# Attention into an MLP on one core: a third buffer for the exps, q and k of the first batch ahead of its values, and the first beacon keys on GpSimd's DMA queue

## The chip, the cores and the metric

The kernel runs on one core of one Trainium2 chip. The metric is the device time of one execution in microseconds (us), as the median of several runs; lower is better. All times inside an execution are counted from the start of the profiled span.

## The reference

Eight batches of causal attention with 16 extra keys ("beacons") ahead of the sequence feed a two-layer MLP. The 4608 rows of the MLP are the 8 x 576 tokens; a row is the 8 heads x 64 values of one token.

```python
B, H, S, Nb, D = (8, 8, 576, 16, 64)
k_all = np.concatenate([beacon_k, k], axis=2)
v_all = np.concatenate([beacon_v, v], axis=2)
scores = scale * np.matmul(q, k_all.transpose(0, 1, 3, 2))
scores = np.where(causal, -1000000000.0, scores)   # the beacons are always visible
a = softmax(scores)
x = np.matmul(a, v_all).transpose(0, 2, 1, 3).reshape(B * S, H * D)
h = x @ w_in                                        # 512 -> 2048
out = (h * sigmoid(1.702 * h)) @ w_out              # 2048 -> 512
```

Inputs and output are float32; the kernel works in float16 with float32 sums.

## The kernel before, in words

**Steps.** A step i is one batch and one pair of heads: 8 x 4 = 32 steps, step i belonging to batch i // 4. For a step, TensorE computes transposed scores (`qk_chunk`, L331) in four chunks of 512, 480, 464 and 208 columns for each of the two heads, into a ring of two PSUM tiles `s`. ScalarE takes the exp of each chunk (`exp_chunk`, L344) into the step's tile `E`, of which there are two. VectorE or GpSimd sets the blocks on the diagonal to zero (`mask_chunk`, L360 or L367). TensorE multiplies by the values (`av_both`, L430, for steps 0 to 3; `av_half`, L401, after that). The values stand beside a column block of ones, so the same matmuls give the softmax sums. VectorE turns these sums round, inverts them, turns them back and multiplies (`z_turn`, `z_recip`, `z_back`, `norm`), which gives `xT`, the transposed input of the MLP.

**MLP.** It runs in nine groups of 512 tokens. `mlp1` (L516) is 64 matmuls into 16 PSUM tiles, each followed by a gelu on ScalarE (L528); `mlp2` (L538) is four blocks of 16 matmuls, whose results are copied out (`mlp2_out`, L549 on ScalarE, L551 on VectorE) and stored. All matmul outputs other than scores share a ring of four PSUM tiles `u`. For every group but the last ones the order on TensorE is written out by `chain` (L939): the 64 matmuls of `mlp1` of the group, then the next attention steps with one block of `mlp2` in each. The first group comes after step 4; its first block of `mlp2` comes in step 7, between the score chunks 1 and 2.

**Loads.** Loads that change the type go through GpSimd's DMA queue, called the software queue here: q and k of the first two batches (`load_qk6`, L146), the values (`load_v`, L218 and L221), `w_in` in four pieces (`load_w1`, L228), q and k of later batches (`load_qk`, L115), `w_out` in four pieces (`load_w2`, L235). The program gives that queue eight semaphores in turn, so a load waits on GpSimd until the eighth load before it has landed. In the first batch q and k of heads 0 and 1 come without a cast on the queues of SyncE and ScalarE (`load_f32`, L155) and are cast in SBUF (`cast_f32`, L165); so do the beacon keys of the first two batches (`load_bk6`, `cast_bk6`, L173 and L179). The beacon keys of the other batches are eight small transfers on SyncE (`load_bk`, L128) and one cast (`cast_bk`, L136). q and k of batches 0 and 1 are transposed on TensorE (`tr_pe`, L190) and copied out (`tr_pe_out`, L198). For later batches VectorE transposes 32 x 32 squares (L253), VectorE or GpSimd put them in order (`tr_order`, L262), and SyncE writes them to DRAM and reads them back in place (L272, L279).

**Planner.** Apart from `chain`, `issue` (L964) decides the order and the engine. It goes through all `Work` items with assumed durations, takes the one that can start first (ties by the due time `key`), and picks the engine that would end first, plus a `BIAS`. What an item `needs` becomes a semaphore wait through the data; what stands in `after` only orders the planner's choice, and puts no wait into the program between two engines.

Of the kernel before, what the change touches and what calls it, by code (L numbers as in the profile page):

```python
# [16 lines left out]
def kernel(  # L17
# [46 lines left out]
    tp = ctx.enter_context(tc.tile_pool(name="tp", bufs=2))  # L64
    ep = ctx.enter_context(tc.tile_pool(name="ep", bufs=2))
    op_ = ctx.enter_context(tc.tile_pool(name="op", bufs=3))
# [15 lines left out]
    def make_keep():  # L82

        nc.gpsimd.affine_select(
            out=keep,
            in_=keep,
            compare_op=ALU.is_ge,
            fill=0.0,
            base=0,
            pattern=[[1, P + Nb]],  # L90
            channel_multiplier=-1,
        )

    w1t = cst.tile([P, NKP, DFF], F16, tag="w1", name="w1")
# [55 lines left out]

    def load_f32(w, eng):

        s = op_.tile([P, 2, S], F32, tag="O", name="O")
        stg[w] = s
        dict(SP=nc.sync, ACT=nc.scalar)[eng].dma_start(  # L155
            out=s.rearrange("p x s -> p (x s)")[0:TP, 0 : 2 * TR * D].rearrange(
                "p (h c) -> p h c", h=2
            ),
            in_=(q, k)[w][0, 0:2].rearrange("h (p t) d -> p h (t d)", t=TR),
        )  # L160

    def cast_f32(w, eng):
        if 0 not in nat6:
            nat6[0] = gp.tile([TP, 2, H, TR * D], F16, tag="g", name="g")
        copy[eng](  # L165
            out=nat6[0][:, w, 0:2, :].rearrange("p h c -> p (h c)"),
            in_=stg[w].rearrange("p x s -> p (x s)")[0:TP, 0 : 2 * TR * D],
        )

    def load_bk6(b):  # L170
        s = sp.tile([P, DMODEL], F32, tag="osb", name="osb")
        stg["b", b] = s
        nc.sync.dma_start(  # L173
            out=s[0:Nb, :].rearrange("n (h d) -> n h d", d=D),
            in_=beacon_k[b].rearrange("h n d -> n h d"),
        )
# [143 lines left out]
    scs = {}  # L320

    def qk_chunk(i, ci):
        b, p = divmod(i, NPAIR)
        qT, kT = qTs[b % 2], kTs[b % 2]
        sc = pss.tile([P, 2, 512], F32, tag="s", name="s")
        scs[(i, ci)] = sc
        o = 0
        for (j, a, e) in CH[ci]:
            for x in range(2):
                r = 64 * x  # L330
                nc.tensor.matmul(  # L331
                    sc[:, x, o : o + e - a],
                    kT[r : r + 64, p, j * P : (j + 1) * P],
                    qT[r : r + 64, p, a:e],
                    start=True,
                    stop=True,
                )
            o += e - a

# [233 lines left out]
    class Buf:  # L573
# [4 lines left out]
    rings = dict(  # L578
        n0=2, n1=2, sq=2, t0=2, t1=2, d0=4, d1=4, qT0=1, qT1=1, kT0=1, kT1=1, vb0=1, vb1=1, s=2, E=2, u=4, O=3,
        zt=2, rt=2, rz=2, xT=RING, g=2, osb=3,  # L580
    )
    SEM, QS = 0.1, 0.1
    SPL, CAP = 2.0, 2.0
    NBOTH = 4
    HWQ = 3

    def use(buf, *ws):
        buf.users += ws
# [4 lines left out]
    placed = {}  # L593
    bkB = None
    pk = {}
    trp = {}
    mkeep = Work("POOL", 0.3, -4.95, make_keep)
    midn = Work("POOL", 0.6, -5.95, lambda: make_identity(nc, ident))

    bk6, stw, cst0 = {}, {}, {}  # L600
    stb = {w: Buf("O") for w in (1, 0, "bk")}
    stw[1] = Work("SP", 0.6, -9, lambda: load_f32(1, "SP"), alloc=stb[1], dma=0.7)
    stw[0] = Work("ACT", 0.6, -9, lambda: load_f32(0, "ACT"), alloc=stb[0], dma=0.7, after=[stw[1]])
    for b in range(NB2):
        ob = Buf("osb")
        x = Work("SP", 0.6, -8 + b, lambda b=b: load_bk6(b), alloc=ob, dma=0.1, after=[stw[1]])
        bk6[b] = Work(
            dict(ACT=0.6, DVE=0.6) if b else dict(ACT=0.6), 0, (-8, 1.5)[b],
            lambda eng, b=b: cast_bk6(b, eng), [x],
        )  # L610
        use(ob, bk6[b])
    g0 = Buf("g")
    for w in (1, 0):
        cst0[w] = Work(
            {("DVE", "ACT")[w]: 0.85}, 0, -8.5 - 0.1 * w, lambda eng, w=w: cast_f32(w, eng),
            [stw[w]],
        )
        use(stb[w], cst0[w])

    def first_loads(b):  # L620
        k0 = 4 * b
        kl = (-6, -4.4)[b]
        gb6 = g0 if b == 0 else Buf("g")
        lds = {(0, 1): cst0[1], (0, 0): cst0[0]} if b == 0 else {}
        got = []
        for (h0, h1) in ((2, 4), (4, H)) if b == 0 else ((0, 4), (4, H)):
            for w in (1, 0):
                x = Work(
                    "POOL", 0.7, kl + 0.1 * h0 + 0.02 * (1 - w) + (h0 == 4),
                    lambda b=b, h0=h0, h1=h1, w=w: load_qk6(b, h0, h1, w),  # L630
                    alloc=None if got else gb6, dma=0.37 * (h1 - h0), after=got[:1],
                )
                got.append(x)
                for p in range(h0 // 2, h1 // 2):
                    lds[(p, w)] = x
        if b == 0:
            for x in cst0.values():
                x.after.append(got[0])
        x = None
# [29 lines left out]
        pk[b] = y  # L669
        if b == 0:  # L670
            bk6[1].after.append(pk[(0, 0, 1)])

    for b in range(B):
# [5 lines left out]
        for g in range(2) if b >= NB2 else ():  # L679
            for w in (1, 0):  # L680
# [17 lines left out]
                for e in range(2):  # L698
                    cp.append(Work(
                        dict(DVE=0.8, POOL=1.3), 0, k0,  # L700
                        lambda eng, b=b, g=g, w=w, e=e: tr_order(b, g, w, e, eng),
                        tr, alloc=tb_ if e == 0 else None, after=cp[:1],
                    ))
                use(sb_, *cp)
                need = []
                if w == 1:
                    if bkB is None:
                        ld4 = [
                            Work(
                                "SP", 1.2, -6 + x, lambda x=x: load_bk(x),  # L710
                                alloc=stb["bk"] if x == 0 else None, dma=0.2,
                            )
                            for x in range(HG)
                        ]
                        for x, y in zip(ld4, ld4[1:]):
                            y.after.append(x)
                        bkB = [Work(dict(ACT=0.85, DVE=0.85, POOL=0.9), 0, 3, cast_bk, ld4)]
                        use(stb["bk"], *bkB)
                    need = [Work(
                        "DVE", 0.25, k0, lambda b=b, g=g: tr_beacon(b, g),  # L720
                        bkB, after=cp[:1],
                    )]
# [12 lines left out]
                placed[(b, g, w)] = pl  # L735
        kv = 4 * b - 1.5 if b >= NB2 else (-5.5, -3)[b]
        for j in range(NJ):
# [26 lines left out]
    avp = {}  # L764
    BIAS = dict(DVE=0.5), dict(ACT=0.7)
    avs = []
    evs = {}
    for i in range(NSTEP):
# [4 lines left out]
        ready = {}  # L773
        for c in range(len(CH)):
            s_ = Buf("s")
            qk_ = Work(
                "PE", CHW[c] / 2400 + 0.05, i + (0, 0.01, 0.4, 0.41)[c],
                lambda i=i, c=c: qk_chunk(i, c),
                [pk[(b, p, 0)], pk[(b, p, 1)], pk[b]] if b < NB2
                else [placed[(b, hf, 0)], placed[(b, hf, 1)]],  # L780
# [6 lines left out]
            ex = Work(  # L787
                "ACT", 0.17 + 2 * CHW[c] / 1200, i + (0, 0.01, 0.4, 0.41)[c],
                lambda i=i, c=c: exp_chunk(i, c), [qk_],
# [6 lines left out]
            nm = sum(1 for (j, a, e) in CH[c] if a == s0s[j])  # L796
            mk = Work(
                dict(DVE=0.46 * nm, POOL=0.41 * nm), 0, i + 0.3,
                lambda eng, i=i, c=c: mask_chunk(i, c, eng), [ex, mkeep],
            )  # L800
            use(Eb, mk)
            for (j, a, e) in CH[c]:
# [5 lines left out]
        if i < NBOTH:  # L808
            for z in (1, 0):
                for half in range(2):  # L810
# [3 lines left out]
                    av = Work(  # L814
                        "PE", sum(hi - lo for (j, lo, hi, col) in mm) / 2400 + 0.15,
                        i + 1.05 + 0.2 * (1 - z) + 0.1 * half,
                        lambda i=i, half=half, z=z: av_both(i, half, z),
                        [r for j in js for r in ready[j]] + vb_, alloc=ub[(half, z)],
                        after=avs[-1:],
# [68 lines left out]

    trp[(0, 1, 1)].after.append(qks[(0, 1)])
    bkB[0].after.append(exps[0][3])  # L890

# [72 lines left out]
    def issue():  # L964
# [7 lines left out]
        while todo:  # L972
            best = None
            for w in todo:
# [18 lines left out]
                for a in w.after:  # L993
                    t = max(t, a.t0)
                eng = min(w.opts, key=lambda e: max(t, free[e]) + w.opts[e] + BIAS[t > 45].get(e, 0))
                t = max(t, free[eng])
# [11 lines left out]
            if eng == "PE":  # L1008
                d += 0.1 * (w.mode != mode)
                mode = w.mode  # L1010
            if w.key >= 1e6 and t < 7:
                d = 0.43
# [65 lines left out]
```

The softmax here doesn't subtract the row's maximum and nothing guards it: scores larger than these inputs give would overflow.

## Time and profile before

| what | value |
|---|---|
| median of 5 runs | 367.94 us (367.52 to 368.38) |
| the profiled execution | 368.5 us |
| its span | 366.8 us |
| TensorE busy | 353.6 us (96%), 2349 matmuls |
| VectorE, ScalarE, GpSimd busy | 249.2 (68%), 228.1 (62%), 152.7 us (42%) |
| software queue (q0) | 18.19 MB |
| queues of SyncE and ScalarE (q1) | 24.55 MB |
| first matmul of the first `mlp1` | at 35.62 us |
| first matmul of the first `mlp2` | at 59.43 us |

The profile has a page with the busy time of each engine (PE is TensorE, PEld its weight loads, DVE VectorE, ACT ScalarE, POOL GpSimd, SP SyncE), the same in 40 slices of the span with the clock that TensorE was granted, the chain of work that ended last, followed back from the end, and the costliest groups of instructions. A line such as `E<-s` reads: the tile E is written from the tile s. Answers of the trace narrow this to a window of time, to an engine or to a tile. A landing is the moment at which all parts of a transfer are done.

### The profile page before, as it was taken

The numbers are of one execution on the slowest core, as the hardware profiler recorded it, in microseconds if no ns is written. First come the engines' busy times: TensorE is split into PE (matmuls) and PEld (weight loads), VectorE is DVE, ScalarE is ACT, GpSimd is POOL, SyncE is SP. The second block draws the span as 40 slices with busy tenths as digits, with TensorE's granted clock in tenths as the row PEclk, the third lists the DMA queues.
The fourth block names the chain that finished last, engine by engine and source line by source line (L and its number), as shares of the span: only waits on it lengthen the run. The fifth ranks groups of instructions, "written<-read, shape, count | busy, mean of one in ns | idle before, by whom it ended". The sixth has DMA issues, their size and how long they took to land.

```text
span 366.8 us, 6133 instructions
## 1 busy us (share of the span) xinstructions
PE 353.6 (96%) x2349; PEld 176.8 (48%) x2349; DVE 249.2 (68%) x421; ACT 228.1 (62%) x335; POOL 152.7 (42%) x264
## 2 busy tenths in 40 slices
PE   7689999999999999999999999999999999999995
PEld 3365444444444444544445864544444454444442
DVE  5547499999999986999599949981995183010021
ACT  4569787648765776677857675677658734616200
POOL 9578567593368244743376236710430010000000
PEclk9969999999999999999999999999999999999999
DMA  9999999994689645894489447921100011000012
GB/s 143 149 206 188 187 236 234 224 110 99 191 231 178 132 126 146 129 168 136 124 113 139 139 141 144 134 87 32 59 30 29 2 57 57 2 29 29 30 57 86
DMA packets 69788, 43.41 MB, mean 118 GB/s; under 512 B 42624, under 2 KB 62080, under 8 KB 69760
## 3 DMA queue, kind: packets, MB, share of 16 engines
q0 software_dynamic: 49152, 18.19, 48.7%
q1 hardware_dynamic: 20400, 24.55, 21.4%
q8 instruction: 18, 0.29, 0.3%
q10 hardware_dynamic: 208, 0.29, 0.3%
q14 instruction: 10, 0.08, 0.1%
HBM read 44.60 MB, written 16.61 MB: 167 GB/s over the span
## 4 chain that ended last, share of the span: by engine, by line
PE 86%; DVE 4%; DMA 3%; ACT 3%; POOL 2%; issue 1%; DVEq 0%; POOLq 0%
PE u L516 34%; PE u L538 34%; PE u L401 9%; PE s L331 7%; DMA g<-in_q_dram 3%; ACT E L344 2%; PE u L430 1%; POOL vb L221 1%; DVE xT L489 1%; PE u L190 1%; DVE rz L480 1%; DVE zt L470 1%; DVE osb L551 1%; DVE O L459 1%; POOL g L146 1%
## 5 line engine op out<-in xcount | busy, mean ns | idle before, releaser
L344 ACT ACTIVATE E<-s 128x1024 f16<-128x1024 f32 (+3 forms) x128 | 103.4, 865 | 48.8 <-PE s L331 46.6
L538 PE MATMUL u<-w,g 128*128 128x512 f16 x576 | 129.2, 379 | 0.6 <-DVE O L459 0.6
L516 PE MATMUL u<-xT,w 128*128 128x512 f16 (+1 forms) x640 | 126.0, 358 | 0.0
L528 ACT ACTIVATE g<-u 128x512 f16<-128x512 f32 x144 | 85.2, 597 | 42.8 <-PE u L516 42.5
L367 POOL TENSOR_SCALAR_AFFINE_SELECT E<-E 128x256 f16<-128x256 f16 (+2 forms) x148 | 63.6, 448 | 84.3 <-ACT E L344 84.1
L516 PEld LDWEIGHTS <-w 128*128 128x128 f16 x640 | 62.1, 98 | 61.3 <-issue 0.9
L538 PEld LDWEIGHTS <-g 128*128 128x128 f16 x576 | 54.5, 98 | 65.4 <-issue 3.6
L551 DVE COPY osb<-u 128x512 f32<-128x512 f32 x30 | 20.5, 683 | 65.3 <-PE u L538 65.0
L459 DVE COPY O<-u 128x240 f32<-128x240 f32 (+1 forms) x84 | 34.8, 439 | 24.5 <-PE u L401 22.1
L262 POOL COPY t<-sq 128x576 f16<-128x576 f16 x21 | 26.7, 1272 | 49.2 <-DVE sq L253 41.5
L401 PE MATMUL u<-E,vb 128*128 128x240 f16 x392 | 46.8, 266 | 0.2
L489 DVE TENSOR_TENSOR xT<-O,rz 64x576 f16<-64x576 f32 x56 | 44.2, 790 | 0.8
L470 DVE STREAM_TRANSPOSE zt<-O 64x576 f32<-64x576 f32 x56 | 43.1, 770 | 1.4
L401 PEld LDWEIGHTS <-vb 128*128 128x128 f16 x392 | 32.2, 98 | 17.3 <-issue 7.6
L331 PE MATMUL s<-qT,kT 64*128 64x80 f16 (+5 forms) x384 | 37.2, 285 | 3.3 <-ACT E L344 2.3
L253 DVE STREAM_TRANSPOSE sq<-n 128x576 f16<-128x576 f16 x48 | 34.9, 747 | 6.7 <-DMA n<-in_k_dram 6.4
L221 POOL DMA_DIRECT2D vb<-in_v_dram x40 | 34.3, 865 | 3.4 <-DMA w<-in_moe_w_in_dram 2.8
L262 DVE COPY t<-sq 128x576 f16<-128x576 f16 x27 | 27.4, 1015 | 0.3
L331 PEld LDWEIGHTS <-kT 64*128 64x128 f16 x384 | 13.3, 94 | 27.6 <-issue 20.0
L480 DVE STREAM_TRANSPOSE rz<-rt 128x576 f32<-128x576 f32 x32 | 24.4, 763 | 0.6
L459 ACT COPY O<-u 128x336 f32<-128x336 f32 (+1 forms) x28 | 10.7, 429 | 2.8 <-PE u L401 2.7
L1043 PE MATMUL u<-wu 128*128 128x512 f16 x29 | 10.4, 461 | 1.3 <-DVE wu L1036 1.3
(44 smaller groups left out, 124.9 us busy)
## 6 DMA issues: line engine op xcount, KB each, us to landing
out_dram<-osb SPq DMA_DIRECT2D x36, 256.0 KB, 2.1
d<-t SPq DMA_DIRECT2D x12, 296.0 KB, 2.8
kT<-d SPq DMA_DIRECT2D x12, 296.0 KB, 3.5
n<-in_k_dram POOLq DMA_DIRECT2D x12, 288.0 KB, 5.2
n<-in_q_dram POOLq DMA_DIRECT2D x12, 288.0 KB, 6.2
d<-t SPq DMA_DIRECT2D x12, 288.0 KB, 2.6
qT<-d SPq DMA_DIRECT2D x12, 288.0 KB, 3.2
vb<-in_v_dram POOLq DMA_DIRECT2D x24, 128.0 KB, 5.7
```

Of the source, the lines that this page charges most:

```text
L221: nc.gpsimd.dma_start(out=vb[r : r + hi - lo, j, :, 0:D], in_=v[b, :, lo:hi, :].rearrange("h n d -> n h d"),)
L262: copy[eng](out=tqk[(b, g, w)][:, e, o : o + S].rearrange("p (r t) -> p r t", t=TPP), in_=sqs[(b, g, w)][:, :, e, :].rearrange("p t r -> p ...
L331: nc.tensor.matmul(sc[:, x, o : o + e - a], kT[r : r + 64, p, j * P : (j + 1) * P], qT[r : r + 64, p, a:e], start=True, stop=True,)
L344: nc.scalar.activation(out=Es[i][:, :, choff[ci] : choff[ci] + w], in_=scs[(i, ci)][:, :, 0:w], func=AFT.Exp, scale=0.125,)
L367: nc.gpsimd.affine_select(out=blk, in_=blk, compare_op=ALU.is_ge, fill=0.0, base=mc, pattern=[[0, 2], [1, w]], channel_multiplier=-1,)
L401: nc.tensor.matmul(u[:, lo:hi], vb[0:kw, j, :, :].rearrange("r h c -> r (h c)")[:, o : o + 2 * D], E[0:kw, x, col : col + hi - lo], start= ...
L459: copy[eng](out=Os[i][:, x, AQ[half] : AQ[half + 1]], in_=avu[(i, x, half)][:, :])
L470: nc.vector.transpose(zst[i][0][64 * x : 64 * x + 64, :, :], Os[i][64 * (1 - x) : 64 * (1 - x) + 64, x, :])
L489: vec[eng].tensor_tensor(out=xT[r : r + 64, p, c : c + S], in0=Os[i][r : r + 64, x, :], in1=zst[i][2][r : r + 64, :], op=ALU.mult,)
L516: nc.tensor.matmul(u[:, o : o + w], w1t[:, kp, nt * P : (nt + 1) * P], xT[:, kp, m : m + w], start=(kp == 0), stop=(kp == NKP - 1),)
L528: nc.scalar.activation(out=gts[g][:, nt, :], in_=hu[(g, nt)][:, :], func=AFT.Gelu_apprx_sigmoid)
L538: nc.tensor.matmul(o[:, :], gts[g][:, nt, mt * P : (mt + 1) * P], w2t[:, nt, :], start=(nt == 0), stop=(nt == NNT - 1),)
```

## The change

- The ring of `E` tiles has three buffers (tile pool and planner).
- q and k of batch 0 all come through `load_qk6` in eight transfers of two heads; `load_f32` and `cast_f32` are gone, and with them ScalarE's only transfer. The due times put all eight in front of most of the values; the transposes of pairs 2 and 3 move up on TensorE.
- The beacon keys of batch 0 are loaded by GpSimd with a cast, straight into `bkn`. Those of batch 1 stay on SyncE. `bkl` and `bkl4` get `after` entries (steps 1 and 2).
- The identity for the transposes is made on GpSimd after the first three transfers.
- In the planner, `BIAS` on ScalarE after 45 us falls from 0.7 to 0.3; steps 0 to 3 have a shorter cost for `av_both`, and its half with the sums no longer needs the values; fillers are priced differently before 5 us. A mask by matmul (`pe_mask`, `neg`, `NMASK`, `CMASK`), `NDM`, `NTP` and `CO0` are added with values that leave them without effect; `make_neg` is not called.

What the new program holds, against the old one: GpSimd's list begins with k and q of heads 0-1, the beacon keys, the identity, k and q of 2-3, the mask constant, k and q of 4-5, the beacon values, two value transfers, k and q of 6-7, three value transfers, and then goes on as before (k and q of batch 1, heads 0-3; w_in; k of heads 4-7; the values of batch 1 with q of heads 4-7 among them; q and k of batch 2; w_out). SyncE's list still begins with the beacon loads (one for batch 1, eight for the others), and none of the first eight of them waits. On TensorE, `mlp1` of the first group stands right behind the last score chunk of step 4, and the first two chunks of step 5 behind it. ScalarE has 14 of the 36 `mlp2_out` copies instead of 6, VectorE 22 instead of 30; of the `av_out` copies VectorE loses 6 to ScalarE; masks go from GpSimd to VectorE (9 operations). The matmuls are the same but for the fillers (26 instead of 29).

```diff
-    ep = ctx.enter_context(tc.tile_pool(name="ep", bufs=2))
+    ep = ctx.enter_context(tc.tile_pool(name="ep", bufs=3))
...
-    def load_f32(w, eng):
...
-    def cast_f32(w, eng):
...
     def load_bk6(b):
+        if b == 0:
+            nc.gpsimd.dma_start(
+                out=bkn[:, 0, :, :], in_=beacon_k[0].rearrange("h n d -> n h d")
+            )
+            return
...
-        qT0=1, qT1=1, kT0=1, kT1=1, vb0=1, vb1=1, s=2, E=2, u=4, O=3,
+        qT0=1, qT1=1, kT0=1, kT1=1, vb0=1, vb1=1, s=2, E=3, u=4, O=3,
...
-    mkeep = Work("POOL", 0.3, -4.95, make_keep)
-    midn = Work("POOL", 0.6, -5.95, lambda: make_identity(nc, ident))
-    stw[1] = Work("SP", 0.6, -9, lambda: load_f32(1, "SP"), alloc=stb[1], dma=0.7)
-    stw[0] = Work("ACT", 0.6, -9, lambda: load_f32(0, "ACT"), alloc=stb[0], dma=0.7, after=[stw[1]])
...
+    mkeep = Work("POOL", 0.3, -5.6, make_keep)
+    midn = Work("POOL", 0.6, MID, lambda: make_identity(nc, ident))
+    bk6[0] = Work("POOL", 0.55, -5.975, lambda: load_bk6(0), dma=0.5)
+    bkl.append(Work("SP", 0.6, -8, lambda: load_bk6(1), alloc=ob, dma=0.1))
+    bk6[1] = Work(dict(ACT=0.6, DVE=0.6), 0, -8, lambda eng: cast_bk6(1, eng), bkl[:1])
...
-        for (h0, h1) in ((2, 4), (4, H)) if b == 0 else ((0, 4), (4, H)):
+        for (h0, h1) in ((0, 2), (2, 4), (4, 6), (6, H)) if b == 0 else ((0, 4), (4, H)):
             for w in (1, 0):
                 x = Work(
-                    "POOL", 0.7, kl + 0.1 * h0 + 0.02 * (1 - w) + (h0 == 4),
+                    "POOL", 0.7, kl + 0.1 * h0 + 0.02 * (1 - w) + (b == 0) * (h0 >= VK) + (b == 1) * (h0 == 4),
...
-        kv = 4 * b - 1.5 if b >= NB2 else (-5.5, -3)[b]
+        kv = 4 * b - 1.5 if b >= NB2 else (-5.55, -3)[b]
...
-    BIAS = dict(DVE=0.5), dict(ACT=0.7)
+    BIAS = dict(DVE=0.5), dict(ACT=0.3)
...
-                        "PE", sum(hi - lo for (j, lo, hi, col) in mm) / 2400 + 0.15,
+                        "PE", sum(hi - lo for (j, lo, hi, col) in mm) / 2400 + 0.06,
...
-                        [r for j in js for r in ready[j]] + vb_, alloc=ub[(half, z)],
+                        [r for j in js for r in ready[j]] + (vb_[-1:] if z else vb_), alloc=ub[(half, z)],
...
-    trp[(0, 1, 1)].after.append(qks[(0, 1)])
-    bkB[0].after.append(exps[0][3])
+    trp[(0, 1, 1)].after.append(qks[(0, CO0[1])])
+    bkl[0].after.append(exps[1][0])
+    bkl4[0].after.append(exps[BKE][0])
...
-            if w.key >= 1e6 and t < 7:
+            if w.key >= 1e6 and t < 5:
```

## The prediction

> **What bounds the kernel now.** I read the page first: TensorE is busy 96% of the span, but not in the first slices, and there the DMA engines are full.
>
> ```profile
> span 366.8 us, 6133 instructions
> ...
> PE   7689999999999999999999999999999999999995
> ...
> PEclk9969999999999999999999999999999999999999
> DMA  9999999994689645894489447921100011000012
> ```
>
> The third digit of PEclk is a clock that fell. Then the chain of waits over the whole span:
>
> ```profile
> 8.59 10.80 DMA g<-in_q_dram
> 19.43 1.65 PE u L190 x36
> ...
> 35.62 13.93 PE u L516 x64
> ...
> 65.92 3.61 PE u L538 x16
> 69.53 0.39 PE s L331 x4
> ```
>
> Until 19.4 the end hangs on one load, q of heads 4 to 7, issued at 8.59 behind the values. From 66 on it is nearly all TensorE, back to back. Between them, the table by stage (busy us of PE, PEld, DVE, ACT, POOL; clock; DMA share; GB/s):
>
> ```profile
> 15.50:18.90 3.40, 1.52 (x20) 0.81 (x20) 1.34 (x3) 3.40 (x5) 2.62 (x6) 1.00 1.32 200
> 18.90:25.70 6.80, 6.26 (x84) 4.39 (x86) 3.10 (x6) 3.78 (x7) 4.24 (x8) 0.50 1.26 205
> 35.60:49.60 14.00, 14.00 (x70) 6.27 (x70) 7.99 (x11) 10.25 (x17) 8.38 (x11) 1.00 1.54 194
> 49.60:59.40 9.80, 8.95 (x103) 4.85 (x99) 9.32 (x21) 9.28 (x14) 8.01 (x12) 1.00 1.24 247
> 59.40:63.10 3.70, 3.70 (x22) 1.60 (x20) 3.48 (x6) 1.86 (x2) 2.95 (x7) 1.00 1.77 223
> 63.10:84.00 20.90, 20.65 (x153) 10.45 (x150) 20.32 (x37) 12.62 (x21) 15.04 (x25) 1.00 1.22 160
> ```
>
> TensorE is half idle from 15.5 to 18.9, then at half clock for 6.8 us. From 49.6 to 59.4, steps 5 to 7, ScalarE and VectorE bind. And the loads never stop: 194 to 247 GB/s up to 59. The last of them that `mlp2` needs is w_out, on GpSimd's queue:
>
> ```profile
> 41.24 1.49 POOL L235 DMA_DIRECT2D w<-in_moe_w_out_dram  x2 [1.15 <-DMA vb<-in_v_dram]
> ...
> 60.63 0.55 POOL L115 DMA_DIRECT2D n<-in_q_dram  x1 [0.56 <-DMA w<-in_moe_w_out_dram]
> ```
>
> ```profile
> L538 PE MATMUL u<-w,g x16: 379/379/389, 59.4 to 62.7; 128*128 128x512 f16 x16
> ...
> DMA to landing us min/median/max: 10.3/13.9/18.4
> ```
>
> The fourth piece of w_out, issued at 41.99, lands 18.4 later, at 60.4. The first `mlp2` block starts at 59.4 and needs that piece at its 13th matmul, at 62.0. So the block has 1.6 us of slack against this queue. This decides how much of a faster start survives.
>
> **What the skill says.** "TensorE: Matmul & The Clock Gate", What's actually happening: the clock halves after an idle window of about 3.4 us, windows run freely, and a busy window brings it back. The trace agrees: 6.8 us at 0.50 is two windows, after one with 1.52 us busy. "DMA: Bandwidth & Descriptors", Issuing engines are not separate DMA queues: all queues share the same 16 engines. The trace agrees: from 45.8 to 60.4 the software queue moves 1.90 MB and the other 1.60 MB, and w_out pieces land 4 us apart, where w_in's landed 2.5 apart (24.8, 27.4, 30.0, 32.5, each issue plus its landing time). The same page, Specifications: transfers under 512 B miss the line rate. The values (128 B written each) cost 1.2 us per 128 KB (batch 1: landings at 39.1 and 40.3), q and k 1.4 per 288 KB (batch 2: 41.6, 43.0, 44.5, 45.9).
>
> **The start.** Before, k and q of heads 0-1 land at 5.0 and 5.7 (0.81 + 4.2 and 4.9) and still need casts (0.83, 0.74). After, the first load is issued at 0.81 instead of 1.55. L146 took 5.3 us to land, beside 2 x 288 KB (float16 size) on the other queues; these are gone, so I take 4.2 to 5.3, k at 5.0 to 6.1 and q 1 us later. First exp at 7.7 to 8.8, against 8.31: no change of weight; two casts and a beacon cast are gone from ScalarE and VectorE, hidden anyway.
>
> The software queue takes on 288 KB (1.45 us) and the beacons (0.2), and starts 0.74 earlier. All of batch 0 was in at 19.4. Summed: eight q/k transfers x 0.72 + values 5.0 (batch 1: 34.25 to 40.7, less 1.43 for a q load between) + 0.2 = 11.0; first packet 2.55 after the issue (4.1 against 1.55), so 3.4; 14.4. SyncE's beacon loads are not deferred: `after` is no wait, and they stand first in its list. Their 1664 packets at 31 ns of an engine (mean of the trace's packet records there), over 16 engines, add 3.2: 17.6. The same sum for before gives 17.3, 2 us short of 19.4, so it is a lower end; range 17.5 to 19.6, taken 17.8: the queue is 1.6 ahead.
>
> Then, with durations of the rows: ScalarE has five steps of exps at 3.13 (15.7), three copies of 0.65 before the last step, 0.4 for beacons and 0.83 for L136: from 7.8 no earlier than 26.7. On TensorE `av_both` of step 0 stands in front of the last score chunk of step 2 and waits for the last values (17.8); with 42 matmuls behind it (2.2) that chunk comes at 20.0 and costs ScalarE 2 us. The third `E` buffer is what lets steps 1 and 2 run their exps before it. Step 3's exps end at 23.8, its last `av_both` at 27, L441 0.53, L476 0.27, L480 0.78, L449 0.82: first `mlp1` at 28.8 (27.5 to 31), against 35.62. W_in's first piece lands at 23. `mlp1` ends at 42.7 instead of 49.55.
>
> **The hole behind it.** `mlp2` followed 9.9 us later (steps 5, 6, half of 7: table load 1.28, ten exp chunks, copies). Two `tr_pe_out` copies now stand between the exps on ScalarE instead of one, +0.65: `mlp2` can start at 53.2, its 13th matmul at 55.8. But w_out's last piece: 60.4 - 1.6, less what the other queue takes. Before, 1.60 MB of it fell into w_out's 14.5 us; now four transfers of about 0.3 MB do, since the third `tr_order` pair is behind step 5 on VectorE: (2.1 + 1.2) / (2.1 + 1.6) x 14.5 = 12.9, -1.6. Half of that taken: 58.0 (57 to 60). So 6.8 us of lead shrink: TensorE stalls 2.2 us inside the block, which ends at 58.0 + 4 x 0.216 + 0.1 = 59.0 against 63.06: **-4.1**. VectorE agrees: from 41.6 to 66 it was never idle for long, its squares start 1.6 earlier and it has one 0.68 copy less; the tile that let `mlp2` go on at 65.92 comes at about 61.
>
> **Clock.** The 2.2 us stall can make a window as empty as the one at 15.5. If it does, a half-clock window of 3.4 us costs 1.7. Even chance: **+0.85**.
>
> **Afterwards** the matmuls are the same. VectorE's two gaps (0.15, 0.39) may close, -0.3. ScalarE's eight more copies: the pattern is in the trace.
>
> ```profile
> 152.84 0.58 ACT L549 COPY osb<-u 128x512 f32<-128x512 f32 x1 [1.82 <-PE u L538]
> ...
> 153.32 1.36 ACT L344 ACTIVATE E<-s 128x928 f16<-128x928 f32 x2
> 154.66 0.60 PE L331 MATMUL s<-qT,kT 64*128 64x512 f16 x8
> ```
>
> The exps end at 154.68, the second chunk wants its buffer at 155.05: 0.37 spare. In eight steps an `av_out` (0.37 to 0.44) now stands between these exps: at most 0.07 each, **+0.5**. Masks moved to VectorE (nine of 0.3) lie before 43 in its idle time. Of GpSimd's moves one needs watching: the fourth `tr_order` pair of batch 2 is now behind the q load that waits for w_out (57 to 58) and behind masks; its write goes out at 63, and q is back at 70.5 (3.3 + 4). Step 10 needs it at 72.7: hidden by 2 us.
>
> Sum: -4.1 + 0.85 - 0.3 + 0.5 = -3.05, taken -3.3 since a stall split by a window's edge costs nothing. Span 363.5; its execution 365.2 (1.7 around the span, as before); the median was 0.56 below the profiled run: **364.6**.
>
> **Rivals.** (A) as above, 362.9 to 366.0: 0.58. (B) The queue is not earlier: beacons and values hold it to the old pace, w_out lands at 60.4 + 0.9 (1.65 added, 0.74 won), the block ends at 62.2, -0.9 and the clock's gain or loss: 366.9, chance 0.14. For it: the 2 us my sum missed. (C) The queue wins 3 us or more and nothing stalls: VectorE binds at -5.2, or ScalarE at -6.2: 362.3, chance 0.12. For it: 1.60 MB of rival traffic. (D) Opposite side: the stall on w_out throws TensorE to half clock for three windows (10.2 us x 0.5 = 5.1) in the saturated stage after 58; -4.1 + 5.1 = +1.0: 368.9. It decides from two and a half windows on. For it: before needed two windows to recover at 92% busy. Against: the stall is shorter than a window. 0.09. (E) ScalarE's copies and step 10's late q return the lead: eight stalls of 0.4, if an `av_out` waits for its matmuls, and 1 us at step 10: 367.9, chance 0.07. That a part does not do what it says holds for the beacons on SyncE only, and is in the sum.
>
> **Numbers.** A measurement of this kernel tells 0.2% (0.74 us). Faster: A, C, and most of B: 0.83. Same: E and the rest of B: 0.08. Slower: D: 0.09. Range 362.3 to 367.4: A, C's upper half and B; outside remain D, E and half of C, near 0.2.
>
> **What would show it.** k of heads 0-1 landing by 6; q of heads 6-7 by 15; last values near 17.8; no clock digit under 9 before 40; first `mlp1` near 28.8; the first `mlp2` block waiting at its 13th matmul for w_out at 58; the rest as before, shifted. Wrong if `mlp1` starts after 32, if w_out lands later than 60.4, or if PEclk shows a new dip after 55 longer than 3.4 us.

## The result and the profile after

The changed kernel takes **371.05 us** (median of 19 runs, 367.87 to 373.56) against 368.07 us for the kernel before (37 runs, 367.49 to 368.72): 1.0071 times as long, 95% interval 1.0054 to 1.0088. I had predicted 364.6 us. The executions of the changed kernel also lie 5.7 us apart, those of the kernel before 1.2. The profiled execution took 369.09 us.

Its page, the same parts as shown of before:

```profile
span 367.4 us, 6162 instructions
...
PE   7989999978999999999999999999999999999995
...
PEclk9599999999999999999999999999999999999999
DMA  8999999997469944894479447920100011000021
```

The loads are no longer full in the tenth slice, so the start did get earlier. But PE has a 7 and an 8 in the ninth and tenth slices (73 to 92 us), where before it had nines. The table by stage shows it (busy us of PE, PEld, DVE, ACT, POOL; clock; DMA share; GB/s):

```profile
45.70:56.30 10.60, 9.75 (x118) 5.45 (x115) 9.22 (x18) 10.02 (x15) 8.60 (x15) 1.00 1.21 234
56.30:60.00 3.70, 3.70 (x19) 1.56 (x19) 3.57 (x8) 2.02 (x3) 3.07 (x5) 1.00 2.05 166
60.00:72.00 12.00, 11.51 (x82) 5.99 (x83) 11.68 (x18) 8.69 (x14) 9.31 (x17) 1.00 1.35 223
72.00:82.20 10.20, 8.63 (x63) 4.45 (x62) 10.08 (x19) 6.08 (x10) 8.27 (x11) 1.00 1.63 203
82.20:85.00 2.80, 1.14 (x6) 0.48 (x5) 2.77 (x6) 2.32 (x3) 2.50 (x5) 1.00 0.35 104
85.00:98.00 13.00, 13.00 (x62) 5.75 (x62) 12.39 (x20) 8.36 (x14) 4.50 (x5) 1.00 0.68 183
```

The first `mlp2` block runs from 56.37 to 59.99, 3.1 us before its old time and without a stall. By 85 all of it is gone: TensorE is idle for 1.6 us between 72 and 82.2 and for 1.7 between 82.2 and 85, and VectorE is busy throughout. The timeline of TensorE there (start, length, what; in brackets the idle time before it and who ended that):

```profile
76.12 0.60 PE L327 MATMUL s<-qT,kT 64*128 64x512 f16 x8 [1.57 <-DMA qT<-d]
...
82.78 1.02 PE L525 MATMUL u<-xT,w 128*128 128x512 f16 x4 [0.57 <-ACT O L468]
84.89 13.11 PE L525 MATMUL u<-xT,w 128*128 128x512 f16 x60 [1.09 <-DVE O L468]
```

The first is q for step 10, read back from DRAM too late. The other two are the second `mlp1`: each of its tiles takes a PSUM buffer `u`, and these are still held by the attention output of step 9 until `av_out` has copied it to `O`. VectorE's timeline says what it did first:

```profile
80.06 2.36 DVE L498 TENSOR_TENSOR xT<-O,rz 64x576 f16<-64x576 f32 x2
82.45 0.75 DVE L254 COPY t<-sq 128x576 f16<-128x576 f16 x1
83.12 1.43 DVE L245 STREAM_TRANSPOSE sq<-n 128x576 f16<-128x576 f16 x2
84.48 1.09 DVE L468 COPY O<-u 128x240 f32<-128x240 f32 x3
```

The matmuls whose results wait were over at 82.2. VectorE first runs a copy and two halves of a square transpose that belong to batch 3, 2.2 us together, and only then the three copies. In the kernel before all four copies of this step were ScalarE's, and TensorE didn't wait (a score chunk of step 10, 0.53 us, also stood between step 9's `av_half` and this `mlp1`; in the new list it comes after the `mlp1`):

```profile
83.16 1.32 ACT L459 COPY O<-u 128x240 f32<-128x240 f32 x4
```

```profile
83.97 2.33 PE L516 MATMUL u<-xT,w 128*128 128x512 f16 x10
```

### The profile page after: what moved, and what is told of

The parts are those of the page before. It is cut to its first block, busy times and chain, and to the rows that moved or that the text cites. A ratio compares the mean times of both kernels' runs of the same rounds, so it can differ in the third digit from the quotient of the medians.

```text
span 367.4 us, 6162 instructions
## 1 busy us (share of the span) xinstructions
PE 353.3 (96%) x2346; PEld 176.0 (48%) x2346; DVE 240.9 (66%) x415; ACT 231.3 (63%) x346; POOL 157.5 (43%) x261
## 4 chain that ended last, share of the span: by engine, by line
PE 76%; DVE 8%; DMA 7%; POOL 3%; issue 2%; ACT 2%; DVEq 0%; POOLq 0%
PE u L547 31%; PE u L525 30%; PE u L410 8%; PE s L327 6%; DMA g<-in_k_dram 4%; DMA n<-in_k_dram 2%; DVE sq L245 2%; ACT E L353 2%; DVE xT L498 2%; DVE zt L479 1%; DMA g<-in_q_dram 1%; POOL vb L213 1%; POOL E L376 1%; DVE rz L489 1%; PE u L182 1%
## 5 line engine op out<-in xcount | busy, mean ns | idle before, releaser
L353 ACT ACTIVATE E<-s 128x1024 f16<-128x1024 f32 (+3 forms) x128 | 105.4, 870 | 32.2 <-PE s L327 30.7
L537 ACT ACTIVATE g<-u 128x512 f16<-128x512 f32 x144 | 84.2, 598 | 41.7 <-PE u L525 41.0
L560 DVE COPY osb<-u 128x512 f32<-128x512 f32 x22 | 15.2, 691 | 66.8 <-PE u L547 66.8
L468 DVE COPY O<-u 128x240 f32<-128x240 f32 (+1 forms) x78 | 33.2, 445 | 33.0 <-PE u L410 30.0
L498 DVE TENSOR_TENSOR xT<-O,rz 64x576 f16<-64x576 f32 x56 | 45.8, 818 | 0.8
L254 POOL COPY t<-sq 128x576 f16<-128x576 f16 x22 | 29.1, 1326 | 39.6 <-DVE sq L245 33.9
L327 PE MATMUL s<-qT,kT 64*128 64x80 f16 (+5 forms) x384 | 38.3, 291 | 3.6 <-DMA qT<-d 1.8
L558 ACT COPY osb<-u 128x512 f32<-128x512 f32 x14 | 8.2, 586 | 29.0 <-PE u L547 29.0
L254 DVE COPY t<-sq 128x576 f16<-128x576 f16 x26 | 22.5, 866 | 0.3
L468 ACT COPY O<-u 128x336 f32<-128x336 f32 (+1 forms) x34 | 13.6, 425 | 2.6 <-PE u L410 1.8
```

The lines of the kernel that those rows point to most:

```text
L254: copy[eng](out=tqk[(b, g, w)][:, e, o : o + S].rearrange("p (r t) -> p r t", t=TPP), in_=sqs[(b, g, w)][:, :, e, :].rearrange("p t r -> p ...
L327: nc.tensor.matmul(sc[:, x, o : o + e - a], kT[r : r + 64, p, j * P : (j + 1) * P], qT[r : r + 64, p, a:e], start=True, stop=not pe_mask(i ...
L353: nc.scalar.activation(out=Es[i][:, :, choff[ci] : choff[ci] + w], in_=scs[(i, ci)][:, :, 0:w], func=AFT.Exp, scale=0.125,)
L468: copy[eng](out=Os[i][:, x, AQ[half] : AQ[half + 1]], in_=avu[(i, x, half)][:, :])
L498: vec[eng].tensor_tensor(out=xT[r : r + 64, p, c : c + S], in0=Os[i][r : r + 64, x, :], in1=zst[i][2][r : r + 64, :], op=ALU.mult,)
L537: nc.scalar.activation(out=gts[g][:, nt, :], in_=hu[(g, nt)][:, :], func=AFT.Gelu_apprx_sigmoid)
```

## The experiments

Five theories appear in the expectations. (1) The lead is given back between 60 and 85 because VectorE and GpSimd have too much to do there, and TensorE no longer sets the time. (2) ScalarE's additional copies cost a little in every group. (3) The start itself varies. After the first four runs two more were formed: (4) the lead is lost at one place, in front of the second `mlp1`, by the order of VectorE's list, and the hole can in addition drop TensorE's clock; (5) VectorE is behind in any order, and what is put back is late for its next reader.

One table holds the readings from all profiles. "Idle" is the idle time of TensorE in front of the first and the second tile of the second `mlp1`; "rest" is from the end of that `mlp1` to the last matmul of the program. Two waits just ahead of these places are not in it: 0.57 in front of the added matmuls of a_fill, and 3.34 in front of step 9's last `av_half` in a_bias07. Times in us.

| kernel | median (range, runs) | ratio to before, 95% | profiled execution | first `mlp1` | idle | second `mlp1` ends | rest |
|---|---|---|---|---|---|---|---|
| before | 368.07 (367.49 to 368.72, 37) | 1 | 368.5 | 35.55 | 0 | 97.96 | 265.15 |
| changed | 371.05 (367.87 to 373.56, 19) | 1.0054 to 1.0088 | 369.09 | 31.68 | 0.57 + 1.09 | 98.00 | 265.03 |
| a_rep | 370.22 (368.75 to 373.29, 8) | 1.0032 to 1.0091 | 371.6 | 32.60 | 0.57 + 1.73 | 100.54 | 265.03 |
| a_pad | 372.83 (371.33 to 373.90, 5) | 1.0104 to 1.0143 | 372.6 | 33.77 | 0.57 + 2.50 | 101.54 | 265.03 |
| a_nomask | 370.42 (368.12 to 372.06, 14) | 1.0042 to 1.0078 | 368.48 | 31.61 | 0.57 + 1.81 | 97.87 | 265.03 |
| b_nomask | 367.52 (366.95 to 368.38, 17) | 0.9979 to 0.9993 | 367.86 | 35.52 | 0 | 97.28 | 265.19 |
| a_ofirst | 367.75 (367.30 to 368.67, 13) | 0.9982 to 0.9998 | 367.3 | 31.14 | 1.66 + 0 | 96.24 | 265.04 |
| a_fill | 369.10 (368.23 to 371.51, 9) | 1.0023 to 1.0066 | 368.81 | 31.47 | 0 + 0.38 | 97.75 | 265.03 |
| a_both | 368.59 (367.14 to 370.97, 14) | 0.9994 to 1.0033 | 368.8 | 32.47 | 1.31 + 0 | 97.75 | 265.04 |
| a_bias07 | 374.61 (371.37 to 376.87, 6) | 1.0121 to 1.0206 | 376.87 | 31.44 | 0 | 106.35 | 264.52 |
| a_ofirst2 | 366.61 (366.10 to 367.62, 6) | 0.9944 to 0.9971 | 367.62 | 32.41 | 0 | 95.42 | 266.17 |
| a_E2 | 373.41 (373.05 to 373.63, 4) | 1.0127 to 1.0153 | 373.37 | 32.72 | 0.53 + 3.81 | 102.55 | 265.25 |
| b_bias03 | 368.76 (368.03 to 369.20, 13) | 1.0005 to 1.0021 | 368.55 | 35.15 | 0 | 98.56 | 264.60 |
| b_E3 | 368.14 (367.59 to 368.61, 12) | 0.9988 to 1.0006 | 367.96 | 35.11 | 0 | 97.71 | 264.86 |

**a_rep: the changed kernel once more.** No edit but an empty comment.

> The changed kernel as it is, for a second profile and more times. Theory 1 (the lead of 3 us at the first mlp2 is real, and is given back between 60 and 85, because VectorE and GpSimd have the transposes of batch 2 left over and step 10 waits for its q): times between 368 and 373; where this execution is longer than the one shown, the added time stands in the wait for qT at step 10 and in front of the second mlp1, and the groups after it take 38.9 each as before. Theory 2 (ScalarE's eight more copies cost a little in every group): the groups after the second mlp1 take 0.3 or more longer each, and the second mlp1 starts where it did before (84.0) or earlier. Theory 3 (the software queue at the start): the first mlp1 itself moves by the 2 to 4 us between executions.

The profiled execution is 2.5 us longer than the one above. Page, timeline of TensorE, and table by stage:

```profile
span 369.9 us, 6162 instructions
...
PE   7988998998999999999999999999999999999995
...
PEclk9999999998999999999999999999999999999999
```

```profile
85.82 14.72 PE L525 MATMUL u<-xT,w 128*128 128x512 f16 x60 [1.73 <-DVE O L468]
```

```profile
83.00:85.80 2.80, 1.02 (x4) 0.38 (x4) 2.77 (x6) 1.89 (x3) 2.52 (x5) 0.98 0.38 105
85.80:89.20 3.40, 3.38 (x9) 1.18 (x9) 3.31 (x8) 0.60 (x1) 1.26 (x2) 0.51 1.04 197
89.20:92.60 3.40, 3.40 (x17) 1.52 (x16) 3.35 (x6) 2.39 (x4) 0.00 (x0) 1.00 0.81 256
```

The hole is 0.64 us longer here, and after it TensorE runs at half clock for one window: 9 matmuls in 3.4 us instead of 17. The same 60 matmuls take 14.72 us instead of 13.11. The sum closes: `mlp1` goes on 0.93 later (85.82 against 84.89), the clock adds 1.61, together 2.54; the executions differ by 371.6 - 369.09 = 2.51. Theory 2 is out for this: the rest of the program takes 265.03 us in both, and 265.15 before. Theory 3 is partly right: the first `mlp1` starts 0.92 later. Theory 1 named both places, but not the clock. The nines of PEclk in the first two slices of this page must not be read as full clock: the trace holds no clock ahead of 17.43, and the matmuls show half clock up to there (twelve of `tr_pe` take 0.69 us at 5.44 and 0.45 at 17.53).

These two profiles do not cover the whole scatter. The mean granted clock is on record for every execution. The three longest of the changed kernel, 373.04 to 373.56, have 0.994 or 0.995 like this one, so there was room for about one window at half clock, worth some 1.7 us of the 4 to 5 us that they lie above 368.7. One of 370.80 has 0.999, no such window on record. What else lengthened these is open.

**a_pad: less lead.**

```diff
         hu[(g, nt)] = u
+        for _ in range(8 if g + nt == 0 else 0):
+            nc.tensor.matmul(u[:, :], wu[:, 0:P], wu[:, :], start=True, stop=True)
```

> The changed kernel with eight idle matmuls of 128x512 (8 x 0.216 = 1.7 us) in front of the first mlp1, so that the lead is cut by 1.7 us before steps 5 to 9. Theory 1: TensorE doesn't set the time between 60 and 85, so the end hardly moves: within 0.5 us of the changed kernel. Theory 2 and any in which TensorE or ScalarE carries the loss: the whole 1.7 us is added (372 to 373).

1.8 us more than the changed kernel's median, 2.6 more than a_rep's on the same chip: the delay comes through, against theory 1. VectorE is full, but its own list starts from what TensorE and ScalarE give it after the first `mlp1`: at 48.57 it waits 3.15 us for an attention output (1.33 at 46.48 in the changed kernel) and then runs on without a gap. TensorE got its buffer 2.2 later (87.09 against 84.89 in the timeline), and the clock fell behind this hole too (14.45 us for the 60 matmuls instead of 13.11). A full engine isn't a fixed bound.

**a_nomask and b_nomask: less work for GpSimd.** The masks of steps 5 to 9 are left out in both kernels, so the upper triangle isn't zeroed there; all other instructions keep their order:

```diff
     def mask_chunk(i, ci, eng):
+        if 5 <= i <= 9:
+            return
```

> The changed kernel without the masks of steps 5 to 9 (left out: the upper triangle isn't zeroed there); all else in the same order. VectorE is rid of some 1.5 us and GpSimd of some 8 us between 50 and 80. Theory 1: the copies for step 10's q go out earlier, the wait for qT falls away, and the kernel keeps most of its lead: 365 to 366.5, and the executions agree within 1.5 us. Theory 2: nothing changes by more than 0.5 us (370 to 371).

> The kernel before, without the masks of steps 5 to 9, as the control: its copies for step 10 are done by 56 and don't stand behind masks, so 367 to 368 by theory 1, a gain of at most 1 us from VectorE; by theory 2 as well.

The changed kernel gained nothing (1.0060 against a_rep's 1.0061), the kernel before 0.14%. The wait for step 10's q was still 1.1 us, the one for `O` 1.81. So the masks in front of GpSimd's copies are not what makes q late. VectorE was hardly relieved: from the norms at 54.70 to step 9's copies at 84.34 its list took 29.64 us, and 29.56 with the masks (54.92 to 84.48), since a `tr_order` copy beside GpSimd's now took 1.18 instead of 0.62 and a wait of 0.40 appeared. So only the part of theory 1 with GpSimd and q fell here; after it I looked at the order of VectorE's list.

**a_ofirst: three instructions behind the copies.** After the planner, in its finished list:

```diff
     order = issue()
+    behind([x for x in sqw[(3, 1, 1)] + cpw[(3, 0, 0)] if x.eng == "DVE"], outs[9])
```

`behind` moves these works, and those that need them (one copy on GpSimd, one write on SyncE), to just after the last of step 9's `av_out`. `sqw`, `cpw` and `outs` hold the squares, the ordering copies and the `av_out` works.

> The changed kernel with three VectorE instructions of batch 3 (a copy t<-sq and the two halves of a square transpose sq<-n, 2.2 us together) placed behind step 9's three copies O<-u instead of ahead of them. Theory 4 (formed from the last profiles: the second mlp1 waits 1.1 to 2.5 us for these copies, the hole of about 2 us that this leaves on TensorE costs its own length, and where a window of the clock falls into it another 1.7 us at half clock; this is the median's 3 us and the spread): the wait for O falls under 0.3 us, no clock digit under 9 near 85, mlp1 takes 14 us in every execution; median 367 to 368.3, spread under 2 us. Theory 5 (VectorE is behind anyway, so what is put behind the copies is late for the next consumer): the wait moves to a later place, median 370 or more.

367.75 us, 0.9990 of before, and the runs lie 1.4 us apart instead of 4.5 to 5.7. One swap of 2.2 us of work on VectorE takes away the whole loss against the kernel before, and the scatter; theory 5 is wrong. It doesn't bring the lead back: of the lead at the first `mlp2` block (it starts at 55.83 here, 3.6 earlier than before) 1.7 us are left at the end of the second `mlp1`, in the shortest of its executions. VectorE and TensorE in the timeline:

```profile
79.42 2.35 DVE L498 TENSOR_TENSOR xT<-O,rz 64x576 f16<-64x576 f32 x2
81.81 1.14 DVE L468 COPY O<-u 128x240 f32<-128x240 f32 x3
82.97 0.80 DVE L254 COPY t<-sq 128x576 f16<-128x576 f16 x1
```

```profile
82.27 13.97 PE L525 MATMUL u<-xT,w 128*128 128x512 f16 x64 [1.66 <-DVE O L468]
```

The wait for `O` did not fall under 0.3 as I had expected: 1.66 us of it now stand ahead of the first tile, behind step 8's norms and a pair of square transposes. That is as long as the two holes of the changed kernel's profile together (0.57 + 1.09). The gain is that the hole ends earlier: VectorE's copies start at 81.81 instead of 84.48, of which the swap is 2.1 us and an earlier start 0.5. After it the 64 matmuls run through at full clock.

**a_fill: more work on TensorE.** The same loop as in a_pad, but six matmuls ahead of the second `mlp1` (`(g, nt) == (1, 0)`).

> The changed kernel with six more matmuls of 128x512 (1.3 us) ahead of the second mlp1's first tile, in time that TensorE would wait anyway; nothing else is changed, so the copies of O come as late as before. Theory 4's second half (the clock): the hole is broken up, the clock keeps its full rate in most executions, and a kernel with more work is faster: median 368.5 to 369.5, few executions above 370.5. If the clock isn't what makes the slower executions: 371 or more, the same spread.

With 1.3 us of matmuls added the kernel is not longer: 1.0044 of before, the changed kernel 1.0071 and 1.0061, with intervals that overlap. So this fits the clock's part but doesn't prove it. The table by stage of its profiled execution shows what the fill does to the hole:

```profile
82.00:83.20 1.20, 1.20 (x6) 0.52 (x6) 1.17 (x3) 1.18 (x1) 1.20 (x3) 1.00 0.06 12
83.20:86.00 2.80, 2.42 (x12) 1.04 (x11) 2.77 (x6) 0.90 (x2) 2.40 (x4) 1.00 0.72 143
86.00:98.00 12.00, 12.00 (x61) 5.33 (x61) 11.17 (x18) 8.27 (x15) 3.62 (x3) 1.00 0.62 189
```

Three of its nine runs are still above 371. The longest of them, 371.51, has a mean granted clock of 1.000, so half clock behind the hole is not what lengthened it. What did is open.

**a_both: q for step 10 as well.** As a_ofirst, and in the finished list GpSimd's second `tr_order` copy of q (batch 2, heads 4 to 7) directly behind its first:

```diff
+    up(cpw[(2, 1, 0)][1], cpw[(2, 1, 0)][0])
```

> As the one with O's copies ahead, and GpSimd's second copy of the fourth pair of batch 2 (for step 10's q) ahead of two masks of 0.6 us each. Theory 4: the wait for qT at step 10 (1.2 to 1.6 us) shrinks by 1.3 as well, median 366 to 367.5, at least as fast as the kernel before. Theory 5: 370 or more.

A miss: 368.59, no better than a_ofirst and scattered over 3.8 us again, though the swap on VectorE is in it. TensorE still waited 0.9 for q. So the swap alone doesn't guarantee a steady kernel. Whether the two masks that were pushed back cost this was not tried.

**a_bias07: ScalarE's surcharge undone.**

```diff
-    BIAS = dict(DVE=0.5), dict(ACT=0.3)
+    BIAS = dict(DVE=0.5), dict(ACT=0.7)
```

> The changed kernel with one part undone: the surcharge on ScalarE in the planner back from 0.3 to 0.7, which puts copies of osb and O back on VectorE. Theory 4 reads the order: here only one half square and a copy t<-sq stand in front of the second mlp1, but VectorE has more copies; the loss is then smaller or the same: 368 to 371. Theory 2 (ScalarE's extra copies are the loss): back to the lead, 365 to 366.5.

Theory 2 would have brought the lead back; instead the kernel is the slowest of all, 374.61 us. My own figure was too low as well. The waits of TensorE (total, times, longest):

```profile
PE u L410 <- DVE osb L560: 6.2, 2, 3.3
PE s L327 <- ACT E L353: 2.0, 4, 0.8
```

It is the same kind of loss at two other places: `u` held by `mlp2`'s results, whose copies are VectorE's again and come after norms, transposes and squares. The clock falls behind these waits as well: 16 matmuls of `mlp2` take 5.16 us instead of 3.63, and the 64 of the second `mlp1` 15.66 instead of 13.97.

**a_ofirst2: the same move, further.** The list given to `behind` also has `sqw[(3, 0, 0)]` and `norms[8]`: two halves of a square transpose and two norms that the second `mlp1` doesn't read.

> The same move as in the kernel with O's copies ahead, carried further: the two halves of q's square transpose for batch 3 (1.45 us) and step 8's two norms (1.6 us), which the second mlp1 doesn't read, go behind step 9's copies of O as well. Theory 4: the wait of 1.7 us that is left in front of the second mlp1 falls to under 0.7, and the lead that comes through grows by 1 to 1.3: median 366.4 to 366.9, under the kernel before. Theory 5: the norms are late for what follows, 367.8 or more.

366.61 us, 0.9958 of before (0.9944 to 0.9971): faster than both kernels. The second `mlp1` starts without a wait, though the first one started 0.7 later than in the changed kernel's profile:

```profile
80.37 1.38 DVE L468 COPY O<-u 128x240 f32<-128x240 f32 x3 [0.33 <-PE u L410]
81.66 1.43 DVE L245 STREAM_TRANSPOSE sq<-n 128x576 f16<-128x576 f16 x2
83.01 1.59 DVE L498 TENSOR_TENSOR xT<-O,rz 64x576 f16<-64x576 f32 x2
```

```profile
81.44 2.75 PE L525 MATMUL u<-xT,w 128*128 128x512 f16 x12
```

Of the gain 1.1 us is lost again in the next group (rest 266.17 instead of 265.03), where a wait of 1.0 for `O` appears.

**a_E2: the third buffer undone.**

```diff
-    ep = ctx.enter_context(tc.tile_pool(name="ep", bufs=3))
+    ep = ctx.enter_context(tc.tile_pool(name="ep", bufs=2))
```

(and `E=3` to `E=2` in the planner's rings)

> The changed kernel with the third buffer of the exps taken away, all other parts kept. The planner then places one copy t<-sq and one half square (1.4 us) ahead of step 9's copies of O, not three instructions. Theory 4: the exps of steps 1 and 2 wait for step 0's av_both again, the first mlp1 starts 1 to 2 us later (33 to 34), and the second mlp1 still waits for O: 369 to 371. If the third buffer is what makes the loss (a rival): 367.5 or less.

373.41, over what I expected. The first `mlp1` starts at 32.72, hardly after the 31.1 to 32.6 of the kernels with three buffers. The loss lies again in front of the second `mlp1`: VectorE has norms, one copy and one half square ahead of step 9's copies, and TensorE gets its buffer 1.95 us later than in the changed kernel's profile. The buffer and the order that the planner makes with it were not separated here.

```profile
86.84 15.71 PE L525 MATMUL u<-xT,w 128*128 128x512 f16 x60 [3.81 <-DVE O L468]
```

```profile
83.00:86.80 3.80, 0.03 (x1) 0.00 (x0) 3.75 (x6) 0.85 (x2) 3.08 (x4) 0.80 0.53 101
86.80:90.20 3.40, 3.36 (x8) 1.17 (x8) 3.31 (x7) 0.60 (x1) 0.20 (x1) 0.50 0.60 174
90.20:93.60 3.40, 3.40 (x13) 1.41 (x12) 3.35 (x6) 1.70 (x3) 1.45 (x1) 0.71 0.28 96
```

With a hole of 3.8 us the clock falls for two windows, 2.6 us on the 60 matmuls, and all four runs are long.

**b_bias03 and b_E3: one part alone in the kernel before.** `BIAS` on ScalarE 0.3; `E` with three buffers.

> The kernel before with one part of the change alone: the surcharge on ScalarE 0.3 instead of 0.7. It moves copies to ScalarE, and its VectorE list has a copy of osb and the halves of a square transpose ahead of one of step 9's copies of O. Theory 4: a wait for O in front of the second mlp1, 368.5 to 370. Theory 2: slower as well, by a wait spread over all groups. If the surcharge helps for itself, as it did between the changed kernel and that with 0.7: 367.5 or less.

> The kernel before with the third buffer of the exps alone. The order on VectorE, ScalarE and TensorE is that of before: 367.7 to 368.4, no change, by every theory in which the loss lies in the order; a faster time would mean that the buffer takes a wait away by itself.

The lower surcharge alone costs 0.13%, with no wait in front of the second `mlp1` (the wait I expected there is one of 1.1 us in front of an `mlp2` block), the buffer nothing. Neither holds the loss: the surcharge of 0.3 costs 0.5 us in one kernel, and going back to 0.7 costs over 3 in the other. It is what the planner makes of the parts together.

## Why the prediction was wrong

**What held.** The start: k of heads 0-1 landed at 5.36 (5.0 to 6.1 predicted), the first exp ran at 8.41 (7.7 to 8.8), batch 0 was in at 18.45 (17.8, range 17.5 to 19.6), w_out's last piece at 57.8 (58.0). With k there was luck: its load was issued at 1.39 and not at 0.81, and landed 4.0 us later, under the 4.2 to 5.3 that I took.

**First `mlp1` at 28.8: mis-sized.** It was 31.68, and 31.1 to 32.6 in eight profiles with this start. The term that was too small is ScalarE's sum from the first exp to step 3's last, with 2 us of waiting in it. ScalarE's timeline:

```profile
11.06 1.42 ACT L353 ACTIVATE E<-s 128x928 f16<-128x928 f32 x2 [0.76 <-PE s L327]
...
15.71 0.94 ACT L353 ACTIVATE E<-s 128x928 f16<-128x928 f32 x1 [0.56 <-PE s L327]
17.18 0.52 ACT L353 ACTIVATE E<-s 128x416 f16<-128x416 f32 x1 [0.53 <-PE s L327]
...
22.69 3.54 ACT L353 ACTIVATE E<-s 128x416 f16<-128x416 f32 x5 [1.59 <-PE s L327]
```

The waits are 3.4 us, and the first exp was 0.6 later than I took, so step 3's exps ended at 26.2, not at 23.8. That the third `E` buffer is what lets these exps run ahead is not borne out: a_E2, without it, starts its first `mlp1` at 32.72, in the one profile there is, and a_rep with it at 32.60. The clock did fall at the start, for three windows (8.3 to 18.5), where I had predicted no digit under 9. TensorE is busy for 10.09 of the 10.5 us from 8.0 to 18.5, and ScalarE's waits are waits for its scores, so the half clock is a likely part of what I had mis-sized. That is not shown: in all eight profiles the clock comes back only at 15.5 to 18.5, so there is none with a start at full clock to compare.

**The stall on w_out and +0.85 for the clock: did not happen.** `mlp2` started at 56.37, not 53.2, so w_out was there in time. The block ended at 59.99 (59.0 predicted): a lead of 3.1 us for 4.1. That this is near is partly luck: a block that starts earlier and waits for w_out was predicted, and one that starts later and doesn't wait came.

**"Afterwards the matmuls are the same", -0.3: this is the step that failed.** I carried the lead from 60 to the end and costed only what I had seen in before: VectorE's small gaps and ScalarE's pattern. I didn't follow VectorE's new list up to the next place where TensorE waits for it. On it three instructions of batch 3 stand ahead of copies that free `u`. The planner put them there because in its own times (assumptions, not measurements) step 9's `av_half` matmuls start at 84.1 to 85.2, and the copies of `O` at 84.9; on the chip the matmuls were over at 82.2, while the copies came at 84.48, as planned. In the profiled execution the lead of 3.1 us was gone at the end of this `mlp1` (98.00 against 97.96); in a_rep's the clock took 1.6 us more. None of the three signs that I had named for being wrong shows in the changed kernel's profile (first `mlp1` by 32, w_out by 60.4, no new dip after 55 in PEclk): none of them looks at this place.

**Step 10's q, "hidden by 2 us": wrong.** I had it back at 70.5; it was written at 65.0 and not at 63, read back from 70.01, and there at 76.1, a wait of 1.57. The two passages took 5.0 and 6.1 us, where I took 3.3 and 4. But the q wait is not what set the end of the hole. From step 4's norms to step 9's copies of `O` VectorE runs without a gap, and it takes the same time whether TensorE waits for q or not: 29.56 us here (54.92 to 84.48), 29.50 in a_fill and 29.55 in a_rep, where step 10's q was in time. With the three instructions behind the copies it takes 27.43 (a_ofirst, 54.38 to 81.81) and 27.60 (a_both). The two ends in the changed kernel's profile and in a_rep's:

```profile
54.92 1.72 DVE L498 TENSOR_TENSOR xT<-O,rz 64x576 f16<-64x576 f32 x2
```

```profile
55.85 1.74 DVE L498 TENSOR_TENSOR xT<-O,rz 64x576 f16<-64x576 f32 x2
85.40 1.09 DVE L468 COPY O<-u 128x240 f32<-128x240 f32 x3
```

**ScalarE's copies, +0.5: wrong.** The rest of the program is 265.03 against 265.15 us.

**The rivals.** D had the right mechanism (a stall, then half clock) at the wrong place and with three windows instead of one; it was given 0.09. E named the late q and a returned lead, for ScalarE's copies, which were innocent. None of them named a copy that frees a buffer.

## What to carry to other kernels

When a planner or a scheduler rebuilds the lists, follow the new order on each engine up to the next point where the bounding engine takes a buffer, and ask which instruction frees that buffer and what now stands ahead of it: here 2.2 us of early work, moved behind such a point, brought the median from 371.05 to 367.75. A hole on TensorE has two prices, its length and, if the clock's window falls on it, another 1.6 us after it. Executions that scatter by whole microseconds were a sign of such a hole here, though the clock explains only part of the scatter. A part undone inside a planned kernel measures the new plan, not the part.

## What the runs showed of the hardware

**Two idle pieces of under 2 us can halve the clock.** The Trainium skill, "TensorE: Matmul & The Clock Gate", Why this matters for your kernels, advises against idle gaps over about 3 us. The traces agree for a_E2 (3.81 us, all runs long), but in a_rep the clock fell after idle stretches of 0.57 and 1.73 with 1.02 us of matmuls between them, while in a_nomask's profile 0.57 and 1.81 left it at 1.00. Here the measurement decides: about 2.3 us of idle time in two pieces is enough in one execution and not in another. Where the windows lie can be read from the traces. In all fourteen profiles the changes of the clock inside a program lie whole multiples of 3.41 us apart (in a_rep it fell at 85.69 and rose at 89.11; the earlier change at 17.43 is 20 windows before). Counted on from these changes, both pieces fall into one window in a_rep, and an edge at 82.62 parts them in a_nomask:

```profile
82.28:85.69 3.41, 1.24 (x7) 0.50 (x6) 3.38 (x5) 2.48 (x4) 3.13 (x6) 1.00 0.46 108
```

```profile
82.62:86.04 3.42, 1.61 (x8) 0.62 (x7) 3.39 (x7) 1.37 (x3) 3.07 (x5) 1.00 0.58 122
```

A window with 1.24 us of matmuls was followed by half clock, one with 1.61 was not. So the window need not be idle, and the prediction took the kernel before too easily as agreeing: the window ahead of its half clock has 1.52 us of matmuls. No busy share parts the cases cleanly: 1.75 us (a_ofirst, 80.35 to 83.76) was not followed by half clock, 2.00 us (a_bias07, 50.09 to 53.50) was.

**A norm on VectorE and a copy on GpSimd hold each other up.** The skill, "SBUF — State Buffer", Who interferes with whom, says that a VectorE instruction with two SBUF inputs contends with a GpSimd instruction that reads SBUF, over ports that work as an exclusive lock. The traces agree. Of the changed kernel's 56 norms (`xT<-O,rz`) the median is 0.755 us and the longest 1.639. The pair of norms at 80.06, just ahead of the late copies, took 2.36 us beside this copy on GpSimd, which itself took 1.60 instead of its median 1.18:

```profile
80.20 1.60 POOL L254 COPY t<-sq 128x576 f16<-128x576 f16 x1 [1.61 <-DVE sq L245]
```

In a_ofirst2 GpSimd's copy comes later and the same two norms take 1.59. So by an estimate from these two durations about 0.8 us of the wait for `O` came from this meeting. No count of busy time shows it, since the 2.36 us count as busy.
